# Gate/up jobs issued whole, the local part ahead of group 1, and the memory read-out behind the filler

## Chip, core and metric

The kernel runs on one core of a Trainium2 chip. The metric is the device time of one execution in microseconds. A run's time is a little longer than the span of its profile, which begins with the first recorded instruction.

## What is computed

One transformer block on 2048 tokens of width 448, in bf16. A condition vector gives six modulation vectors; the block is an attention with memory, then a gated MLP, each behind a modulated LayerNorm and each added to its input:

```python
mod = (_silu(c) @ w_mod).reshape(c.shape[0], 6, 1, -1)
h = _layernorm(x, axis=-1) * (1 + ca) + sa
x = x + ga * _A_ref(h, A_wq, A_wk, A_wv, A_wo, A_beta)
h = _layernorm(x, axis=-1) * (1 + cb) + sb
x = x + gb * _B_ref(h, B_w_gate, B_w_up, B_w_down)
```

The attention has 16 heads of 28 and works on 4 segments of 512 tokens. In each segment the output of a head is a mix of two parts. The local part is a causal softmax attention in the segment. The memory part reads a matrix M and a vector z, which sum phi(k) v and phi(k) over the earlier segments, with phi(q):

```python
num = jnp.einsum('bhld,bhde->bhle', pq, M)
den = jnp.einsum('bhld,bhd->bhl', pq, z)[..., None] + 1e-06
o = g * (num / den) + (1.0 - g) * a_dot
M = M + jnp.einsum('bhld,bhle->bhde', pk, vs)
```

The MLP computes `(sigmoid(h @ w_gate) * (h @ w_up)) @ w_down`, with 1792 inner columns.

## The kernel before

The order of the instructions is written out by hand. One list of jobs, `fill`, holds the PE work that isn't softmax attention: projections, memory updates, wo tiles, gate/up jobs and down tiles, each with an estimated cost in ns. A main loop (lines 697 to 737) goes over the 4 segments `s`, in each over 4 units `hc` (four heads each), and in each unit over three logits groups `g`. After each group `run_fill` (582) takes jobs from the list until the pace of the segment is used up. `later` and `tick` (76, 88) put off small operations of DVE, POOL and ACT by an estimated time, so that they stand later in the queues.

- `logits` (401) makes one group: matmuls for four heads side by side into the one PSUM tile `lg` (four banks), then one exponential on ACT (417). Groups 0 and 1 are 512 columns wide per head (group 1 as 384 + 128), group 2 is 256. A new group can start only when the exponential of the one before has read `lg`. After group 0 from segment 1 on, `phi` (359) makes an exponential of the unit's queries on ACT, and two DVE operations (365, 366) later.
- `mask` (423) runs on POOL.
- `pv` (428) is the local part of the unit before: 40 matmuls `acc` (439), then on DVE r1 (445, 446), t1 (451) and ou (452).
- `mem_read` (456) is the memory read-out of the unit before: 4 matmuls `mem` (463), then on DVE r2 (466, 467) and t2 (470). `otr` (481) issues the transpose of the result to oT on the SP queue.
- `wo_tile` (490): 4 matmuls `pwo`, on DVE the sum with x (497), the LN statistics, and later xn (267, 270); its transpose to hT goes over SP (276). The modulation (280) follows on DVE.
- `gate_up` (512) makes the first part of a job for two of the 14 column blocks: 6 gate matmuls (519), then four short ones (524), two of them side by side in two halves of the array, the last rows of gate and of up; two tanhs on ACT (527). `gate_up2` (531) makes the other 6 up matmuls (536) and the two products fT on DVE (539).
- `down` (541): 14 matmuls `dps`, then the sum with x on DVE (549) and the output transfer.

Everything but `lg` shares four PSUM buffers (`ps_m`). A new tile takes one whose tile was released, and its first matmul waits for the operation that read it last. The projections' q and v copies are on ACT (342, 353), the k copy on DVE (344). `prep_b1` (591) puts off seven scalings of w_down by DVE (603).

Because the gate/up job is in two, a logits group and its exponential stand between its first part and its second: line 703 takes `gate_up2` right after a group, and `run_fill` goes on to a first part when a second part was the last it took. In segment 0, `prev` has no memory to read.

Of the kernel before, what the change touches and what calls it, by code (L numbers as in the profile page):

```python
# [17 lines left out]
def kernel(  # L18
# [23 lines left out]
    NFC = F // P  # L42
# [33 lines left out]
    def later(ns, fn, tag):  # L76
        deferred.append((clock[0] + ns, len(deferred), fn, tag))

    def run_deferred(pick):
        while True:  # L80
            due = [d for d in deferred if pick(d)]
            if not due:
                return
            d = min(due, key=lambda d: d[:2])
            deferred.remove(d)
            d[2]()

    def tick(ns):
        clock[0] += ns
        run_deferred(lambda d: d[0] <= clock[0])  # L90
# [154 lines left out]
    hT_of = {}  # L245
    MM, MV, TR = 216, 190, 60
    GU = 14 * MM + 200
# [111 lines left out]
    def phi(src, wait, tag, then=None):  # L359
        e = work.tile([P, L], BF16, tag="e", bufs=5, name="e")  # L360
        nc.scalar.activation(e[:], src, AF.Exp)

        def fin():
            r = work.tile([P, L], BF16, tag="r", bufs=2, name="r")
            nc.vector.tensor_scalar(r[:], src, 0.0, 1.0, op0=ALU.max, op1=ALU.add)
            nc.vector.tensor_tensor(e[:], e[:], r[:], ALU.min)
            if then:
                then(e)
        later(wait, fin, tag)
        return e  # L370
# [28 lines left out]
    pT_of, pq_of, ou_of, oT_of = {}, {}, {}, {}  # L399

    def logits(s, hc, g):
        u = (s, hc)
        qT, kT = qT_of[s], kT_of[s]
        if g == 0:
            pT_of[u] = pipe.tile([P, 4, PTW], BF16, tag="pT", bufs=2, name="pT")
        pT = pT_of[u]
        lg = ps_lg.tile([P, 4, 512], F32, tag="lg", name="lg")
        w0 = OFF[KB_GROUPS[g][0]]
        wid = 0
        for kb in KB_GROUPS[g]:  # L410
            nq = L - kb * P
            for hs in range(4):
                r = slice(HP * hs, HP * hs + Dh)
                nc.tensor.matmul(lg[:, hs, wid:wid + nq], lhsT=kT[r, hc, kb * P:(kb + 1) * P],  # L414
                                 rhs=qT[r, hc, kb * P:L], start=True, stop=True, tile_position=(HP * hs, 0))
            wid += nq
        nc.scalar.activation(pT[:, :, w0:w0 + wid], lg[:, :, 0:wid], AF.Exp, scale=scale)  # L417
        if g == 0 and s > 0:
            pq_of[u] = phi(qT[:, hc, :], 3600, ("pq", u))
        for kb in KB_GROUPS[g]:  # L420
            later(2600, lambda kb=kb: mask(pT, kb), ("mask", u))

# [33 lines left out]
    def mem_read(s, hc):  # L456
        u = (s, hc)
        mem = m_f32("mem")
        memv = mem[:].rearrange("p (t h e) -> p t h e", h=4, e=HP)
        need(("pq", u), ("rm", s))  # L460
        pq = pq_of.pop(u)
        for qb in range(TPS):
            nc.tensor.matmul(memv[:, qb, :, 0:ME], lhsT=pq[:, qb * P:(qb + 1) * P], rhs=rm_of[s][:, hc, :, :],  # L463
                             start=True, stop=True)
        r2 = work.tile([P, TPS, 4], F32, tag="r2", bufs=2)
        nc.vector.scalar_tensor_tensor(r2[:], memv[:, :, :, Dh], 1e-6, cb(1, hc), op0=ALU.add, op1=ALU.mult)
        nc.vector.reciprocal(r2[:], r2[:])
        t2 = work.tile([P, TPS * 4, Dh], F32, tag="t2", bufs=2)
        t2_of[u] = t2
        nc.vector.tensor_tensor(t2[:], num(mem), bc(r2), ALU.mult)  # L470
# [10 lines left out]
    def otr(s, hc):  # L481
        ou = ou_of.pop((s, hc))
        if hc == 0:
            oT_of[s] = pipe.tile([P, NHC, TPS, P], BF16, tag="oT", bufs=1, name="oT")
        nc.sync.dma_start_transpose(oT_of[s][:, hc, :, :], ou[:].rearrange("p t h e -> p (t h e)"))
# [21 lines left out]

    fT_of = {}

    half = {}  # L510

    def gate_up(s, f0):
        h = hT_of[("2", s)]
        fcs = (f0, f0 + 1)
        fs = [slice(fc * P, (fc + 1) * P) for fc in fcs]
        gp = [m_f32("gps") for _ in fcs]
        for g, f in zip(gp, fs):
            for k in range(3):
                nc.tensor.matmul(g[:, 0:L], lhsT=wg_sb[:, k, f], rhs=h[:, k, :], start=(k == 0), stop=False)  # L519
        up = [m_f32("ups") for _ in fcs]  # L520
        tts = []
        for g, u, f in zip(gp, up, fs):
            for dst, r, first in ((g, 0, False), (u, LW, True)):
                nc.tensor.matmul(dst[:, 0:L], lhsT=wgu_sb[r:r + LW, f], rhs=h[r:r + LW, 3, :], start=first,  # L524
                                 stop=not first, tile_position=(r, 0))
            tt = work.tile([P, L], F32, tag="tt", bufs=3)
            nc.scalar.activation(tt[:], g[:, 0:L], AF.Tanh, scale=0.5)  # L527
            tts.append(tt)
        half[0] = (s, fcs, up, fs, tts)

    def gate_up2():
        s, fcs, up, fs, tts = half.pop(0)
        h = hT_of[("2", s)]
        for fc, u, f, tt in zip(fcs, up, fs, tts):
            for k in range(3):
                nc.tensor.matmul(u[:, 0:L], lhsT=wu_sb[:, k, f], rhs=h[:, k, :], start=False, stop=(k == 2))  # L536
            ft = pipe.tile([P, L], BF16, tag="fT", bufs=NFC + 2, name="fT")
            fT_of[(s, fc)] = ft
            nc.vector.scalar_tensor_tensor(ft[:], tt[:], 1.0, u[:, 0:L], op0=ALU.add, op1=ALU.mult)  # L539
# [28 lines left out]
    def h2_jobs(s):  # L568
        return [(0, lambda: need(("ln2", s)))]

    def gu_jobs(s):
        jobs = []
        for fc in range(0, NFC, 2):
            jobs += [(GU - 6 * MM, lambda fc=fc: gate_up(s, fc)), (6 * MM, gate_up2)]
        return jobs

    def down_jobs(s):
        return [(NFC * MV, lambda t=t: down(s, t)) for t in range(TPS)]
# [1 line left out]
    fill = deque()  # L580

    def run_fill(ns):
        fn = None
        while fill and (ns > 0 or fn is gate_up2 and fill[0][0] == GU - 6 * MM):
            cost, fn = fill.popleft()
            fn()
            tick(cost)
            ns -= cost
        return ns
# [61 lines left out]
    m = [mem_jobs(s) for s in range(3)]  # L651
# [39 lines left out]
    def cost(jobs):  # L691
        return sum(cst for cst, _ in jobs)
# [3 lines left out]
    debt = 0.0  # L696
    for s in range(NSEG):
        for hc in range(NHC):
            prev = (s, hc - 1) if hc else (s - 1, NHC - 1)
            for g in range(3):  # L700
                logits(s, hc, g)
                tick(450)
                if fill and fill[0][1] is gate_up2:
                    fill.popleft()[1]()
                    tick(6 * MM)
                    debt -= 6 * MM
                if prev[0] > 0 and g == 0:
                    mem_read(*prev)
                    tick(250)
                if prev[0] >= 0 and g == 1:  # L710
                    pv(*prev)
                    tick(1000)
                if s >= 1 and hc == 1 and g == 0:
                    gj = gu_jobs(s - 1)
                    tail = list(fill)
                    print("left", s, cost(tail), len(tail))
                    fill.clear()
                    while tail and tail[0][1] is gate_up2:
                        fill.append(tail.pop(0))
                    for w in wo_jobs(s - 1):  # L720
                        fill.append(w)
                        if tail and s > 1:
                            fill.extend(tail[:2])
                            tail = tail[2:]
                    fill.extend(tail)
                    if s >= 2:
                        dj = down_jobs(s - 2)
                        fill.extend(dj[:3] + h2_jobs(s - 1) + dj[3:] + gj)
                    else:
                        fill.extend(h2_jobs(s - 1) + gj[:2] + m[2][0:1] + gj[2:10] + m[2][1:] + gj[10:])  # L730
                    pace[0] = (cost(fill) - KEEP[s] * GU) / (12 if s < 3 else 9)
                debt = run_fill(pace[0] + debt)
                if debt > 0:
                    print("dry", s, hc, g, debt)
                    debt = 0.0
                if prev[0] >= 0 and g == 2:
                    otr(*prev)
    last = NSEG - 1
    dj = down_jobs(last - 1)
    mem_read(last, NHC - 1)  # L740
    run_fill(2000)
    pv(last, NHC - 1)
    tick(1100)
    run_fill(1500)
    otr(last, NHC - 1)
    run_fill(3500)
    for c, fn in wo_jobs(last):
        fn()
        tick(c)
    fill.extend(dj)  # L750
    run_fill(1e9)
    for c, fn in h2_jobs(last) + gu_jobs(last) + down_jobs(last):
        fn()
# [30 lines left out]
```

## Time and profile before

| | us |
|---|---|
| median of 3 runs | 268.51 |
| the runs | 267.37, 268.51, 268.67 |
| the profiled execution | 267.37 |
| its span | 265.7 |

The profile has a page and answers drawn from its trace. A page's first part gives the busy time of each engine, the chain is the work that ended last, followed back from step to step. A timeline's row has the start, the time, the engine, the line, the operation with its output and inputs, and in brackets how long the engine was idle before it and what ended the wait. PE is TensorE, PEld its weight loads, DVE is VectorE, ACT is ScalarE, POOL is GpSimd, SP the queue of SyncE. A matmul row is drawn to its modelled end: matmuls of 512 columns take 380 ns in it, but follow each other after 215.

The stages of the span: up to about 28 us loading, LN and the first projections; to 90 us projections of the later segments as filler; to 201 us gate/up jobs, wo and down tiles of the segment before; after 201 us no logits are left, and the MLP of segment 3 is the end.

### The profile page before, as it was taken

To read this page: it belongs to the slowest core of one execution; us is meant where nothing else is said; L and a number is where in the kernel's file an instruction comes from. 1 tells how busy PE (TensorE), PEld (TensorE's weight loads), DVE (VectorE), ACT (ScalarE), POOL (GpSimd) and SP (SyncE) were. 2 spreads that over 40 slices of the span, in tenths; PEclk is the share of its full clock that TensorE was granted. 3 is DMA by queue.
4 is the path that set the end of the run, shared out by engine and by line. 5 is a ranking of instruction groups with operands and counts; after the bars stand their busy time and mean duration, and the time that the engine had idled before them with its cause. 6 is when DMAs were issued, how large, how long until landed. Compare 5 with 4: busy or idle time off the path is not lost.

```text
span 265.7 us, 5242 instructions
## 1 busy us (share of the span) xinstructions
PE 241.1 (91%) x2030; PEld 113.3 (43%) x2054; DVE 183.4 (69%) x431; ACT 137.8 (52%) x169; POOL 70.8 (27%) x130
## 2 busy tenths in 40 slices
PE   7798799979496999898999999899999999999995
PEld 2434344534242443453544343445443445433352
DVE  5789898956489868888976575896765568444421
ACT  0569589948436697883617658533572210133300
POOL 3229323522244313343422131243230013000000
PEclk9999999988999999999999999999999999999999
DMA  5999568296901202300232000013200003300011
GB/s 153 278 238 271 177 139 172 38 208 158 184 22 42 54 8 42 60 21 20 58 62 55 20 20 2 20 23 94 57 1 20 22 0 61 89 0 0 2 35 35
DMA packets 40992, 19.66 MB, mean 74 GB/s; under 512 B 29704, under 2 KB 40072, under 8 KB 40968
## 3 DMA queue, kind: packets, MB, share of 16 engines
q1 hardware_dynamic: 39320, 18.36, 30.7%
q10 hardware_dynamic: 1648, 0.98, 1.4%
q8 instruction: 16, 0.26, 0.4%
q14 instruction: 8, 0.07, 0.1%
HBM read 10.67 MB, written 1.84 MB: 47 GB/s over the span
## 4 chain that ended last, share of the span: by engine, by line
PE 43%; DVE 6%; ACT 2%; issue 2%; DMA 1%; POOL 0%; DVEq 0%
PE dps L545 14%; PE ups L536 10%; PE gps L519 9%; PE gps L524 4%; PE acc L439 2%; PE pwo L494 2%; DVE fT L539 1%; PE lg L414 1%; ACT pT L417 1%; DVE ot L549 1%; DMA hT<-xn 1%; ACT tt L527 1%; DVE t L451 1%; DVE hT L280 1%; PE mem L463 1%
## 5 line engine op out<-in xcount | busy, mean ns | idle before, releaser
L417 ACT ACTIVATE pT<-lg 128x2048 bf16<-128x2048 f32 (+1 forms) x48 | 76.8, 1600 | 32.6 <-PE lg L414 32.5
L425 POOL TENSOR_SCALAR_AFFINE_SELECT pT<-pT 128x512 bf16<-128x512 bf16 x64 | 42.6, 681 | 68.9 <-ACT pT L417 68.9
L527 ACT ACTIVATE tt<-gps 128x512 f32<-128x512 f32 x56 | 30.4, 595 | 56.1 <-PE gps L524 56.1
L539 DVE SCALAR_TENSOR_TENSOR fT<-tt,ups 128x512 bf16<-128x512 f32 x56 | 36.9, 685 | 31.4 <-PE ups L536 27.5
L545 PE MATMUL dps<-wd_sb,fT 128*128 128x448 bf16 x224 | 43.7, 352 | 0.1
L536 PE MATMUL ups<-hT,wu_sb 128*128 128x512 bf16 x166 | 40.7, 381 | 0.2 <-issue 0.2
L519 PE MATMUL gps<-hT,wg_sb 128*128 128x512 bf16 x154 | 39.8, 379 | 0.8 <-issue 0.2
L545 PEld LDWEIGHTS <-fT 128*128 128x128 bf16 x224 | 21.6, 98 | 20.1 <-issue 0.2
L263 POOL TENSOR_SCALAR rs<-mv 128x1 f32<-128x1 f32 (+2 forms) x21 | 5.4, 256 | 72.7 <-DVE mv L260 69.4
L519 PEld LDWEIGHTS <-wg_sb 128*128 128x128 bf16 x168 | 15.9, 98 | 17.7
L536 PEld LDWEIGHTS <-wu_sb 128*128 128x128 bf16 x168 | 14.2, 98 | 21.1 <-issue 7.1
L259 DVE BATCH_NORM_STATS2 st<-x_sb 128x6 f32<-128x448 bf16 x32 | 19.7, 617 | 3.4 <-DMA x_sb<-in_A_x_dram 2.8
L414 PE MATMUL lg<-qT,kT 28*128 28x512 bf16 (+3 forms) x256 | 17.4, 305 | 3.1 <-ACT pT L417 2.8
L339 PE MATMUL pq<-hT,wq_sb 128*128 128x512 bf16 x60 | 16.8, 379 | 3.4 <-DVE hT L298 2.8
L524 PE MATMUL ups<-hT,wgu_sb 64*128 64x512 bf16 x56 | 17.6, 381 | 2.1 <-DVE x_sb L497 1.5
L439 PEld LDWEIGHTS <-pT 128*128 128x128 bf16 x640 | 17.5, 96 | 4.3 <-issue 2.9
L267 DVE TENSOR_SCALAR xn<-x_sb,mv,rs 128x448 bf16<-128x448 bf16 x32 | 16.0, 519 | 4.6 <-POOL rs L264 4.6
L439 PE MATMUL acc<-vt,pT 128*128 128x29 bf16 x640 | 18.6, 175 | 0.5 <-ACT tt L527 0.5
L549 DVE TENSOR_TENSOR ot<-dps,x_sb 128x448 bf16<-128x448 f32 x16 | 9.8, 619 | 11.4 <-PE dps L545 9.4
L339 PE MATMUL pq<-hT,wk_sb 128*128 128x512 bf16 x61 | 16.3, 380 | 0.9 <-ACT qT L342 0.5
L524 PE MATMUL gps<-hT,wgu_sb 64*128 64x512 bf16 x56 | 17.0, 381 | 0.1
L351 PE MATMUL pv<-wv_sb,hT 128*128 128x448 bf16 x64 | 15.1, 380 | 2.0 <-DVE kT L344 2.0
(89 smaller groups left out, 256.6 us busy)
## 6 DMA issues: line engine op xcount, KB each, us to landing
wm<-in_w_mod_dram SPq DMA_DIRECT2D x5, 392.0 KB, 8.2
out_dram<-ot SPq DMA_DIRECT2D x16, 112.0 KB, 1.7
x_sb<-in_A_x_dram SPq DMA_DIRECT2D x3, 448.0 KB, 4.7
wd_sb<-in_B_w_down_dram SPq DMA_DIRECT2D x3, 448.0 KB, 9.5
wg_sb<-in_B_w_gate_dram SPq DMA_DIRECT2D x3, 448.0 KB, 3.7
wu_sb<-in_B_w_up_dram SPq DMA_DIRECT2D x3, 448.0 KB, 5.9
wm<-in_w_mod_dram ACTq DMA_DIRECT2D x1, 392.0 KB
wo_sb<-in_A_wo_dram SPq DMA_DIRECT2D x4, 98.0 KB
```

The source lines that it names most:

```text
L259: nc.vector.bn_stats(st[:], self.srcs[i])
L339: nc.tensor.matmul(pq[:, 0:L], lhsT=head_cols(w_sb, k, hc), rhs=h[:, k, :], start=(k == 0), stop=(k == NK - 1))
L414: nc.tensor.matmul(lg[:, hs, wid:wid + nq], lhsT=kT[r, hc, kb * P:(kb + 1) * P], rhs=qT[r, hc, kb * P:L], start=True, stop=True, tile_posi ...
L417: nc.scalar.activation(pT[:, :, w0:w0 + wid], lg[:, :, 0:wid], AF.Exp, scale=scale)
L425: nc.gpsimd.affine_select(out=blk, in_=blk, compare_op=ALU.is_ge, fill=0.0, base=0, pattern=[[0, 4], [1, P]], channel_multiplier=-1)
L439: nc.tensor.matmul(accv[:, qb, hs, 0:ME], lhsT=pT[:, hs, c0:c0 + P], rhs=vt[:, kb, hc * 4 + hs, 0:ME], start=(kb == 0), stop=(kb == qb))
L519: nc.tensor.matmul(g[:, 0:L], lhsT=wg_sb[:, k, f], rhs=h[:, k, :], start=(k == 0), stop=False)
L524: nc.tensor.matmul(dst[:, 0:L], lhsT=wgu_sb[r:r + LW, f], rhs=h[r:r + LW, 3, :], start=first, stop=not first, tile_position=(r, 0))
L527: nc.scalar.activation(tt[:], g[:, 0:L], AF.Tanh, scale=0.5)
L536: nc.tensor.matmul(u[:, 0:L], lhsT=wu_sb[:, k, f], rhs=h[:, k, :], start=False, stop=(k == 2))
L539: nc.vector.scalar_tensor_tensor(ft[:], tt[:], 1.0, u[:, 0:L], op0=ALU.add, op1=ALU.mult)
L545: nc.tensor.matmul(dp[:, 0:D], lhsT=fT_of[(s, fc)][:, t * P:(t + 1) * P], rhs=wd_sb[:, fc, :], start=(fc == 0), stop=(fc == NFC - 1))
```

## The change

The diff has these parts.

1. `gate_up` makes the whole job again, first the 6 gate matmuls, the four short ones and the tanhs, then the 6 up matmuls and the products. `gate_up2`, the jobs of two pieces, and what handles them in `run_fill` and the loop are gone.
2. The local part of the unit before (`pv`) stands ahead of the logits of group 1, not behind.
3. The memory read-out (`mem_read`) stands behind the filler of group 0, not ahead of it.
4. The DVE part of phi for the queries is put off by 4500, not 3600.
5. At the end: a fill time of 6000 in place of 1500, of 3000 in place of 3500, and two of the four down tiles of segment 2 are put on the list ahead of the last wo tiles.

```diff
-            pq_of[u] = phi(qT[:, hc, :], 3600, ("pq", u))
+            pq_of[u] = phi(qT[:, hc, :], 4500, ("pq", u))
...
-        half[0] = (s, fcs, up, fs, tts)
-
-    def gate_up2():
-        s, fcs, up, fs, tts = half.pop(0)
-        h = hT_of[("2", s)]
         for fc, u, f, tt in zip(fcs, up, fs, tts):
...
-        jobs = []
-        for fc in range(0, NFC, 2):
-            jobs += [(GU - 6 * MM, lambda fc=fc: gate_up(s, fc)), (6 * MM, gate_up2)]
-        return jobs
+        return [(GU, lambda fc=fc: gate_up(s, fc)) for fc in range(0, NFC, 2)]
...
-                logits(s, hc, g)
-                tick(450)
-                if fill and fill[0][1] is gate_up2:
-                    fill.popleft()[1]()
-                    tick(6 * MM)
-                    debt -= 6 * MM
-                if prev[0] > 0 and g == 0:
-                    mem_read(*prev)
-                    tick(250)
                 if prev[0] >= 0 and g == 1:
                     pv(*prev)
                     tick(1000)
+                logits(s, hc, g)
+                tick(450)
...
                 if prev[0] >= 0 and g == 2:
                     otr(*prev)
+                if prev[0] > 0 and g == 0:
+                    mem_read(*prev)
+                    tick(250)
...
     pv(last, NHC - 1)
     tick(1100)
-    run_fill(1500)
+    run_fill(6000)
     otr(last, NHC - 1)
-    run_fill(3500)
+    fill.extend(dj[:2])
+    run_fill(3000)
     for c, fn in wo_jobs(last):
         fn()
         tick(c)
-    fill.extend(dj)
+    fill.extend(dj[2:])
```

The number of matmuls, and of instructions on the other engines, is the same. The order of PE's jobs in three places (G is a job's first part, U its second, lg0 to lg2 the groups, q and k projections, v the value projections):

```
segment 1, its first wo tiles
before: lg0 mem wo wo wo lg1 acc wo k q lg2 k q lg0 mem k v v lg1 acc v v
after:  lg0 wo wo wo mem acc lg1 wo k q lg2 k q lg0 k v v mem acc lg1 v v

then the first gate/up jobs
before: G lg2 U lg0 mem G lg1 U acc G lg2 U G lg0 U mem lg1 acc G lg2 U dM lg0 mem wo G lg1 U acc wo
after:  GU lg2 lg0 GU mem acc lg1 GU lg2 GU lg0 mem acc lg1 GU lg2 dM lg0 wo GU mem acc lg1 wo

after the last logits group
before: lg2 GU G mem U G acc U GU GU wo wo wo wo, four down tiles, seven GU, four down tiles
after:  lg2 GU mem GU acc GU GU GU wo wo wo wo, four down tiles, seven GU, four down tiles
```

More of the change, by code (lines that the diff above doesn't have):

```diff
@@ L508 @@
     fT_of = {}
-    half = {}
     def gate_up(s, f0):
@@ L582, in run_fill @@
     def run_fill(ns):
-        fn = None
-        while fill and (ns > 0 or fn is gate_up2 and fill[0][0] == GU - 6 * MM):
+        while fill and ns > 0:
             cost, fn = fill.popleft()
@@ L717 @@
                     fill.clear()
-                    while tail and tail[0][1] is gate_up2:
-                        fill.append(tail.pop(0))
                     for w in wo_jobs(s - 1):
@@ L722 @@
                         if tail and s > 1:
-                            fill.extend(tail[:2])
-                            tail = tail[2:]
+                            fill.append(tail.pop(0))
                     fill.extend(tail)
@@ L729 @@
                     else:
-                        fill.extend(h2_jobs(s - 1) + gj[:2] + m[2][0:1] + gj[2:10] + m[2][1:] + gj[10:])
+                        fill.extend(h2_jobs(s - 1) + gj[:1] + m[2][0:1] + gj[1:5] + m[2][1:] + gj[5:])
                     pace[0] = (cost(fill) - KEEP[s] * GU) / (12 if s < 3 else 9)
```

## The prediction

> **What bounds the kernel now.** I read the page's busy shares first, then the chain that ended last, then the timelines of PE, DVE and ACT from 70 us on.
>
> ```profile
> PE 241.1 (91%) x2030; PEld 113.3 (43%) x2054; DVE 183.4 (69%) x431; ACT 137.8 (52%) x169; POOL 70.8 (27%) x130
> PE 43%; DVE 6%; ACT 2%; issue 2%; DMA 1%; POOL 0%; DVEq 0%
> ```
>
> PE bounds the kernel. The second line is the chain, which is only traced back to 119 us; in that part PE is on it nearly everywhere, and DVE and ACT only where PE waits. The number of matmuls doesn't change, so the change is worth what it does to PE's waits. These are the waits that it touches (PE timeline; in brackets the idle time and its releaser):
>
> ```profile
> 72.72 2.33 PE L494 MATMUL pwo<-wo_sb,oT 128*128 128x448 bf16 x10 [1.87 <-DMA oT<-ou]
> ...
> 84.38 0.92 PE L351 MATMUL pv<-wv_sb,hT 128*128 128x448 bf16 x4 [0.94 <-DVE kT L344]
> 86.35 0.92 PE L351 MATMUL pv<-wv_sb,hT 128*128 128x448 bf16 x4 [1.05 <-DVE kT L344]
> ...
> 93.93 0.40 PE L414 MATMUL lg<-qT,kT 28*128 28x512 bf16 x4 [0.25 <-ACT pT L417]
> ...
> 101.56 0.39 PE L524 MATMUL ups<-hT,wgu_sb 64*128 64x512 bf16 x1 [0.52 <-DVE t L451]
> ...
> 108.13 0.40 PE L414 MATMUL lg<-qT,kT 28*128 28x384 bf16 x8 [0.78 <-ACT pT L417]
> ...
> 123.24 0.37 PE L524 MATMUL ups<-hT,wgu_sb 64*128 64x512 bf16 x1 [0.75 <-DVE x_sb L497]
> ...
> 153.07 0.40 PE L414 MATMUL lg<-qT,kT 28*128 28x384 bf16 x8 [0.78 <-ACT pT L417]
> ...
> 161.52 0.40 PE L414 MATMUL lg<-qT,kT 28*128 28x512 bf16 x4 [0.25 <-ACT pT L417]
> ...
> 171.14 0.37 PE L524 MATMUL ups<-hT,wgu_sb 64*128 64x512 bf16 x1 [0.80 <-DVE x_sb L497]
> ...
> 202.31 0.37 PE L463 MATMUL mem<-rm,e 128*128 128x116 bf16 x4 [0.47 <-ACT tt L527]
> ...
> 206.28 1.15 PE L439 MATMUL acc<-vt,pT 128*128 128x29 bf16 x40 [0.47 <-ACT tt L527]
> ```
>
> The bracket understates a wait, because the matmul before it is drawn to its modelled end. I therefore use starts: four L524 matmuls take 0.53 us in the chain (0.32 and 0.21), but 1.44 at 100.44 to 101.88, 1.65 at 121.89 to 123.54 and 1.80 at 169.65 to 171.45. Those waits are 0.9, 1.1 and 1.3.
> The Trainium skill ("Trainium Kernel Development and Optimization", Performance Expectations) calls matmul busy time a bad metric because matmuls are pipelined. By the brackets the three removals are 2.1 us and the sum below +2.7; by the starts they are 3.3 and the sum +1.5.
>
> Durations used, all from this trace: one gate/up job 3.23 (1.29 gate + 0.53 + 1.40 up), memory read-out 0.22 to 0.32, local part 1.05, one wo tile 0.76, the dM matmuls 0.94. Exponentials: 1.88 and 1.03. Tanh: 0.55. From the start of a 256-wide logits group (134.06) to its exponential is 0.34 (134.40); with 1.02 for it and 0.04 until PE goes on, the next group can start 1.40 after it.
>
> **To 72.7 us: nothing.** The local part goes ahead of group 1, ACT's total stays the same, and the first wo matmuls wait for the oT transposes, which SP issues from 51.18 to 68.97 without a gap. Those stand in the same order on SP, but for one pk transpose that passes one hT transpose. Without that cover, a reordering of ACT would cost up to its 0.74 at 46.83. I take 0.
>
> **73 to 92 us, the DVE queue: +2.1.** DVE works here almost without a pause:
>
> ```profile
> 70.00:80.00 10.00, 7.53 (x85) 3.82 (x83) 7.63 (x21) 5.61 (x6) 4.55 (x9) 1.00 0.45 46
> 80.00:90.00 10.00, 7.66 (x84) 3.88 (x82) 9.49 (x24) 6.63 (x8) 4.25 (x7) 1.00 0.24 56
> ```
>
> (Columns: stretch, length, PE, PEld, DVE, ACT, POOL busy, clock, DMA.) Before, the first read-out's three DVE instructions (70.51 to 71.55) and one w_down scaling (71.55) ran while PE waited for oT. Afterwards both stand behind the first wo sums: 1.03 + 0.55 = 1.58 us more ahead of the kT copies, for which PE waits at 84.38 and 86.35. The second read-out (86.76) moves behind the third kT copy, ahead of the last hT modulation, and the first gate tile of the next job gets its PSUM buffer. Walking the queue, the first gate matmul moves from 90.06 to about 91.7: +1.65. The modulations also need the last hT transpose, for which the walk uses the median landing, 2.6 us from issue. From the end of the last xn copy to the first modulation it took 3.6 and 3.7 at 133.04 to 136.63 and 180.66 to 184.36, with an output transfer ahead on SP, which doesn't stand there now; that would make it +2.6. I take 2.1, halfway, because SP's issues stand close here too. Lower bound -0.5: the kT waits of 2.0 go, but hT's landing keeps most of it.
>
> **Group 2 straight before group 0 (first gate/up unit): +0.8.** Before, 1.40 us of up matmuls lay between the two and 0.25 was still waited. Now nothing does: 1.40 minus the group's 0.22 is 1.2, less 0.4 for what is waited and lost there today.
>
> **Group 2 with only dM or one wo tile behind it: +0.7.** 1.40 minus 0.22 minus 0.94 is 0.25; with 0.76 it is 0.42. Before, the 1.40 us of up matmuls covered both.
>
> **Read-out and local part right after a gate/up job: +0.9.** Their PSUM buffers are those of the two tanh inputs (L527). After group 0, ACT has its exponential (1.88) and one of phi (0.6) ahead of the tanhs; the first time also one of kT. The walk gives 0.7 there, and 0.1 at each of the two later jobs of that kind. Bounds 0.3 and 1.5.
>
> **Waits at 101 and 108: -1.1.** 0.9 goes, because PE has a whole job between a local part and the last L524. The 0.8 at 108 stays as 0.65: 1.27 of read-out and local part lie behind group 0 instead of up matmuls and read-out, and the exponential no longer stands behind two tanhs.
>
> **Waits at 123 and 171: -0.2.** 1.1 + 1.3 go. In their place, t1 (L451) now has the read-out's 1.03 and phi's 0.7 ahead of it on DVE, and the last up tile gets the buffer of the same job's first gate tile, so it waits for its tanh: 0.85 to 1.45 each, depending on whether xn and its copy take 0.5 (as at 178.09) or 1.13 (165.80 to 166.93). I take 1.1 each.
>
> **144 to 162: -0.5.** 0.2 at 153 and 0.3 at 161, where a whole job now covers group 2's exponential.
>
> **After the last logits group: -1.2.** Four waits go: 0.16, 0.47, 0.47 and about 0.3 at 210.5. The read-out and the local part follow whole jobs, whose tanhs are done. Bounds -1.4 and -0.7. The other numbers of fill time and the two down tiles put in early change nothing: in the built order, gate/up jobs use the time up, and all four down tiles still stand behind the last wo tile. They cover the last LN as before, just so: its modulation starts at 228.08, the gate matmuls at 228.96. If two had gone ahead, 5.3 us of that cover would be missing.
>
> Sum: 2.1 + 0.8 + 0.7 + 0.9 - 1.1 - 0.2 - 0.5 - 1.2 = **+1.5 us**. The profiled execution took 267.37 (span 265.7 and 1.7 around it) and would take 268.9. It is the fastest of the three runs; their median is 268.51, so I predict **270.0**.
>
> **The clock.** The granted clock is 1.00 from 70 to 90 us in the rows above, with waits of 0.94, 1.05 and 1.87 in them, so I take no loss from the new waits.
> The Trainium skill ("TensorE: Matmul & The Clock Gate", Part 1) puts PE at half rate after an idle window of about 3.4 us; by an estimate from that page one such window would add 1.7 us to the sum. No wait that I expect is that long.
>
> **Rivals.**
> - *Even.* The hT transposes land in 2.6 us and xn is quick: 1.65 and -0.7 for the terms 2.1 and -0.2, so +0.6, and with the tanh term at its lower 0.3 it is 0.0: 268.5 to 269.1. For it: I walked the queue to 1.65. Against: xn took 0.69, not 0.36, where POOL worked beside it. 0.36.
> - *Faster.* One mechanism: DVE's queue is less full than I walk it, as the wo sums and LN steps pack closer. The kT copies are then on time at 84, and t1 at 122 and 170. The 73 to 92 term is its lower bound, -0.5, and at 123 and 171 only the tanh wait of 0.3 each is left: -1.8. Sum -2.7: 265.8. It decides from the point where DVE idles over 1.6 us between 74 and 86, but the trace shows it idle there only 0.2. 0.12.
> - *DVE behind for longer.* The backlog reaches the next LN and the gate jobs at 140 and 188 wait for hT: 2.6 for the first term, 0.5 at 123 and 171, tanh 1.5: +3.3 to +4: 272. Against: hT is ready 2 us before 140 and 0.7 before 188. 0.15.
> - *As forecast*, +1 to +2.5: 0.37.
>
> By these cases, with the even one's edge and the forecast's lower edge inside 0.5% (1.34 us, about what a measurement of this kernel tells from no change: the three runs lie 0.49% apart): faster 0.12, same 0.38, slower 0.50. The range leaves out most of the faster case (0.09) and what the last one has above 272.5 (0.06): 266.9 to 272.5; the likeliest case's own is 269.5 to 271.
>
> **What would show it.** The first gate matmul 1.6 to 2.6 later than 90.06, behind DVE; a wait of about 1.2 between group 2 and group 0 after it; waits of mem and acc on tt; no wait of PE between the last logits and the last wo. The prediction is wrong if the first gate matmul comes before 91, or if the time past 188 doesn't shrink by about 1.

## The result, and the profile after

The changed kernel took 271.95 us (median of 4 runs, 271.51 to 272.43), the kernel before, run beside it, 267.94 (4 runs, 267.26 to 268.67): a ratio of 1.015 (1.0111 to 1.0188). Repeated (e5 below) it took 270.33 against 268.28: 1.0082 (1.0058 to 1.0105). So it is slower, by 2 us or by 4; most of the difference between the two goes with PE's clock, as e1 shows. The profiled execution took 272.43 us with a span of 270.7. Busy shares and the chain of its page:

```profile
PE 245.1 (91%) x2029; PEld 115.4 (43%) x2054; DVE 184.1 (68%) x431; ACT 137.7 (51%) x169; POOL 70.0 (26%) x130
...
PE 62%; DVE 16%; DMA 9%; ACT 7%; issue 4%; SPq 1%; POOL 1%; ACTq 0%; DVEq 0%
```

PE still bounds it and does the same matmuls, but is busy 4 us longer; three more stretches at half clock in this execution (see e1) can account for that. DVE's part of the chain went from 6% to 16%; the two aren't quite alike, because this chain is traced back to the start. The waits that answer to those shown of before, in the timeline of PE:

```profile
75.17 3.35 PE L494 MATMUL pwo<-wo_sb,oT 128*128 128x448 bf16 x10 [2.57 <-DMA oT<-ou]
...
82.93 1.04 PE L339 MATMUL pq<-hT,wq_sb 128*128 128x512 bf16 x4 [0.91 <-DVE t L470]
...
90.12 0.37 PE L463 MATMUL mem<-rm,e 128*128 128x116 bf16 x4 [0.81 <-DVE kT L344]
...
94.13 1.47 PE L517 MATMUL gps<-hT,wg_sb 128*128 128x512 bf16 x5 [0.70 <-DVE t L470]
...
99.01 0.40 PE L414 MATMUL lg<-qT,kT 28*128 28x512 bf16 x4 [1.13 <-ACT pT L417]
...
102.96 0.37 PE L463 MATMUL mem<-rm,e 128*128 128x116 bf16 x4 [0.22 <-ACT tt L525]
...
114.41 0.40 PE L414 MATMUL lg<-qT,kT 28*128 28x384 bf16 x8 [0.73 <-ACT pT L417]
...
128.69 0.37 PE L522 MATMUL ups<-hT,wgu_sb 64*128 64x512 bf16 x1 [0.22 <-ACT tt L525]
...
136.76 0.82 PE L439 MATMUL acc<-vt,pT 128*128 128x29 bf16 x26 [0.50 <-POOL pT L425]
...
160.90 0.40 PE L414 MATMUL lg<-qT,kT 28*128 28x384 bf16 x8 [0.73 <-ACT pT L417]
```

In the kernel before, the first gate matmul has no wait:

```profile
90.06 1.46 PE L519 MATMUL gps<-hT,wg_sb 128*128 128x512 bf16 x5
```

Three things are to be seen. The first gate matmul comes at 94.13 instead of 90.06, and the last thing that it waits for is the read-out's t (L470), whose PSUM buffer it takes; a q projection waits for the same at 82.93. Group 2 is followed straight by group 0, and PE waits 1.13 for the exponential. The waits for x_sb and t1 at 101, 123 and 171 are gone or shorter, and past the last logits no PE wait is drawn any more. The DVE timeline shows why the read-out is late. Before, its t (L470) comes ahead of the first wo sum (L497):

```profile
71.00 0.62 DVE L470 TENSOR_TENSOR t<-mem,r 128x448 f32<-128x448 f32 x1
...
73.58 0.62 DVE L497 TENSOR_TENSOR x_sb<-pwo,x_sb 128x448 bf16<-128x448 f32 x1 [1.42 <-PE pwo L494]
```

Afterwards:

```profile
79.86 0.62 DVE L497 TENSOR_TENSOR x_sb<-pwo,x_sb 128x448 bf16<-128x448 f32 x1
...
82.25 0.62 DVE L470 TENSOR_TENSOR t<-mem,r 128x448 f32<-128x448 f32 x1
...
91.99 1.06 DVE L280 TENSOR_SCALAR hT<-hT,cols 128x512 bf16<-128x512 bf16 x3 [0.79 <-DMA hT<-xn]
...
93.45 0.62 DVE L470 TENSOR_TENSOR t<-mem,r 128x448 f32<-128x448 f32 x1
93.99 0.60 DVE L280 TENSOR_SCALAR hT<-hT,cols 128x512 bf16<-128x512 bf16 x1
```

Its instructions stand behind three wo sums with their LN steps (the third ends at 81.9), and the second one stands between the hT modulations that the gate matmuls need.

### The profile page after: what moved, and what is told of

Same layout as the page of the kernel before. It is cut to its first block, busy times and chain, and to the rows that moved or that the text cites. A ratio compares the mean times of both kernels' runs of the same rounds, so it can differ in the third digit from the quotient of the medians.

```text
span 270.7 us, 5234 instructions
## 1 busy us (share of the span) xinstructions
PE 245.1 (91%) x2029; PEld 115.4 (43%) x2054; DVE 184.1 (68%) x431; ACT 137.7 (51%) x169; POOL 70.0 (26%) x130
## 4 chain that ended last, share of the span: by engine, by line
PE 62%; DVE 16%; DMA 9%; ACT 7%; issue 4%; SPq 1%; POOL 1%; ACTq 0%; DVEq 0%
PE dps L538 15%; PE ups L529 13%; PE gps L517 12%; PE pq L339 6%; PE gps L522 5%; DMA wm<-in_w_mod_dram 4%; ACT pT L417 4%; PE lg L414 3%; PE acc L439 3%; DMA hT<-xn 3%; PE pwo L494 2%; DVE st L259 2%; DMA oT<-ou 2%; DVE xn L267 2%; DVE x_sb L497 1%
## 5 line engine op out<-in xcount | busy, mean ns | idle before, releaser
L425 POOL TENSOR_SCALAR_AFFINE_SELECT pT<-pT 128x512 bf16<-128x512 bf16 x64 | 41.5, 664 | 76.3 <-ACT pT L417 76.3
L517 PEld LDWEIGHTS <-wg_sb 128*128 128x128 bf16 x168 | 15.2, 98 | 19.4 <-issue 1.7
L339 PE MATMUL pq<-hT,wq_sb 128*128 128x512 bf16 x60 | 18.0, 410 | 3.9 <-DVE hT L298 2.6
L439 PEld LDWEIGHTS <-pT 128*128 128x128 bf16 x640 | 18.3, 96 | 2.7 <-issue 1.3
L494 PE MATMUL pwo<-wo_sb,oT 128*128 128x448 bf16 x64 | 15.2, 374 | 2.7 <-DMA oT<-ou 2.6
L267 DVE TENSOR_SCALAR xn<-x_sb,mv,rs 128x448 bf16<-128x448 bf16 x32 | 15.4, 498 | 0.4 <-POOL rs L264 0.4
```

The lines of the kernel that those rows point to most:

```text
L339: nc.tensor.matmul(pq[:, 0:L], lhsT=head_cols(w_sb, k, hc), rhs=h[:, k, :], start=(k == 0), stop=(k == NK - 1))
L425: nc.gpsimd.affine_select(out=blk, in_=blk, compare_op=ALU.is_ge, fill=0.0, base=0, pattern=[[0, 4], [1, P]], channel_multiplier=-1)
L439: nc.tensor.matmul(accv[:, qb, hs, 0:ME], lhsT=pT[:, hs, c0:c0 + P], rhs=vt[:, kb, hc * 4 + hs, 0:ME], start=(kb == 0), stop=(kb == qb))
```

## The experiments

All times are medians; e1 to e4, e5 to e8 and e9 to e12 ran on one chip each, with the kernel before among them (268.12, 268.28 and 268.98 us).

### How far do runs of one kernel lie apart?

**e1**: the kernel before, unchanged.

> The kernel before, unchanged, to see how far its time and its mean granted clock move by themselves. The changed kernel's profile is 2.45 us behind already at the first wo tiles (75.17 for 72.72), 0.7 of it before 28 us where the order is the same, with granted clocks of 0.83 to 0.93 from 10 to 40 us where the profile of before has 1.00. Theory A (the early clock is chance, the same for both kernels): the mean clock here spreads from about 0.975 to 0.995 and the time by 1 to 2 us. Theory B (the changed order makes the clock fall): the clock here stays at 0.99 or more in nearly all runs, ratio 1.000.

268.79 us against 268.12, ratio 1.0017 (0.9986 to 1.0049): no difference, as it must be. But its 12 runs go from 266.87 to 270.25, and 22 of the other set's 23 from 266.40 to 269.77 (one took 270.54): 1.4% in all, not the 0.49% that I had read from three runs. Part of this goes with the mean granted clock, which moves in steps. Below is e9's trace by single microseconds (columns: stretch, length, PE, PEld, DVE, ACT, POOL busy, PE's clock, DMA share, GB/s), where the matmuls had just resumed at 108.94 after a wait of 1.72 us:

```profile
109.00:110.00 1.00, 1.00 (x37) 0.79 (x37) 0.06 (x1) 1.00 (x2) 0.59 (x1) 1.00 0.62 123
110.00:111.00 1.00, 0.95 (x20) 0.57 (x18) 0.46 (x3) 1.00 (x1) 0.00 (x0) 0.90 0.37 82
111.00:112.00 1.00, 1.00 (x4) 0.30 (x2) 0.96 (x2) 0.26 (x1) 0.67 (x2) 0.50 0.27 58
...
114.00:115.00 1.00, 1.00 (x6) 0.29 (x3) 0.27 (x1) 0.20 (x1) 0.00 (x0) 0.89 0.22 46
```

The clock is either 1.00 or 0.50, and a half-rate stretch is 3.4 us long here and in every profile of this case (once, in e12, two follow each other), so one costs at most 1.71 us of matmul work. It begins after PE is at work again here, and mostly. In the 14 profiles one began in, or within 3.4 us behind, 22 of the 26 PE waits of 2.0 us or more and 9 of the 38 from 1.2 to 2.0 (without the wait that every run starts with).

Which waits do it isn't chance alone. In every profile the stretches begin on a grid of 3.413 us, counted from the first record of the clock: in the changed kernel's profile this record is at 4.64, and its stretches, at 11.47, 28.54, 59.26 and 76.32, begin 2, 7, 16 and 21 steps later. I leave out the 39 steps that hold the one-column matmuls of the condition vector. Of the others, PE was drawn idle for 47% or more (the share that parts the two kinds best here) in 26, and 24 of these were followed by a step at half rate; of the 1016 with less idle time none was. So a wait counts by how much of one step it fills: e9's wait of 1.72 us fell nearly whole into the step from 107.38 to 110.80, and half rate began at 110.80. The grid starts at another point in every execution, and that is what is left to chance.

The Trainium skill ("TensorE: Matmul & The Clock Gate", Part 1) has this as a gate at half or full rate, judged over free-running windows of about 3.4 us, and asks for one idle window of that length; the length of a stretch and the grid agree, but here a window about half idle has been enough.

A mean clock of 0.994, 0.987, 0.981 and 0.975 is then about one, two, three and four stretches: (1 − clock) × span / 1.71. For the kernel before the mean times of 10, 23, 29 and 7 runs with so many are 267.4, 268.1, 268.7 and 269.2 us. Fitted by a line, one costs 0.61 us and not 1.71; some fall where PE would wait anyway (e8 shows such a place). The line explains about a third of the runs' variance; the rest stays open. This allows a second reading of each kernel below: **its time less that of the kernel before with as many stretches** ("at equal clock", with twice the standard error). For the changed kernel that is +2.65 ± 0.34 over both sets of runs (10 runs): +2.92 in the first, whose runs had three or four stretches, and +2.47 in e5, with one or two. It leaves out what a kernel's own waits do to the clock: the mean number of stretches is 2.5 in the kernel before, 2.4 in the changed one, but 4.2 in e4 and 4.8 in e12.

### Which part of the change costs the time?

**e3**: the read-out goes back ahead of the filler, the rest stays.

```diff
                 logits(s, hc, g)
                 tick(450)
+                if prev[0] > 0 and g == 0:
+                    mem_read(*prev)
+                    tick(250)
...
-                if prev[0] > 0 and g == 0:
-                    mem_read(*prev)
-                    tick(250)
```

> The changed kernel with the memory read-out back ahead of the filler of group 0. Theory (the read-out's DVE work in the full DVE queue at 73 to 92 costs 1.6 us, and its wait for tanh 0.7, and 0.2 at each of two later jobs): 1.5 to 2.5 us faster than the changed kernel, ratio to before 1.006 to 1.010. Rival (DVE isn't what delays the first gate matmul, but the clock and the later oT landing): ratio 1.013 to 1.016.

267.86 us, ratio 0.9988 (0.9959 to 1.0018); at equal clock +0.01 ± 0.24. With the read-out early the whole loss is gone: the other four parts together are worth nothing. In PE's timeline the first gate matmul has no wait any more. The second read-out now waits 1.40 for phi (L366), whose DVE part part 4 puts off further; before, it waited 0.35, and not for phi:

```profile
73.15 2.32 PE L494 MATMUL pwo<-wo_sb,oT 128*128 128x448 bf16 x10 [1.39 <-DMA oT<-ou]
...
83.67 0.39 PE L463 MATMUL mem<-rm,e 128*128 128x116 bf16 x4 [1.40 <-DVE e L366]
...
90.22 1.61 PE L517 MATMUL gps<-hT,wg_sb 128*128 128x512 bf16 x5
```

From the first of these rows to the last it is 17.07 us; before it was 17.34, in the changed kernel 18.96. So the wait for phi costs nothing in this stretch. Whether the other parts would gain without part 4 wasn't tried.

**e6** and **e7**: only the two read-outs that fall beside the first wo tiles go back ahead (e6), or only those two stay late (e7).

```diff
e6, behind the logits, and then in the late place (e7: the two conditions exchanged)
+                if prev[0] > 0 and g == 0 and prev in ((1, 0), (1, 1)):
+                    mem_read(*prev)
+                    tick(250)
...
-                if prev[0] > 0 and g == 0:
+                if prev[0] > 0 and g == 0 and prev not in ((1, 0), (1, 1)):
```

> The changed kernel with only the two read-outs between 70 and 92 us (of segment 1, units 0 and 1) ahead of the filler; the other ten stay behind it. Theory (the DVE queue at 73 to 92 us and the wait for oT ahead of it are the cost): recovers 2.5 to 3.5 of the 4 us, ratio 1.002 to 1.006. Rival (the waits of later read-outs for tanh, and later DVE queues, cost the most): recovers 1 or less, ratio 1.011 or more.

> The complement: only those two read-outs behind the filler, the other ten ahead of it. Theory: loses 2.5 to 3.5 us against the version with all read-outs early, ratio 1.008 to 1.012. Rival: 1.000 to 1.004. If the two parts don't add up to the 4 us, they act on each other.

e6 took 268.69, ratio 1.0012 (0.999 to 1.0034), at equal clock +0.78 ± 0.38. e7 took 269.94, ratio 1.0061 (1.0037 to 1.0085), at equal clock +1.79 ± 0.40. They add up: 0.78 + 1.79 = 2.57 of 2.65. The two read-outs at the wo tiles are worth 1.8 us, the other ten 0.8. I had expected 2.5 to 3.5 for the two, since I counted from 4 us, which held what the clock had added.

**e5**: the changed kernel again, to stand beside them.

> The changed kernel, unchanged, on this chip and beside the others: 271 to 272.5 us, ratio 1.011 to 1.016. Its mean granted clock, 0.975 to 0.981 in four runs, against 0.974 to 0.994 in 35 runs of the kernel before: if the late read-out draws the clock down, it stays at or below 0.985 here; if that was chance, it spreads as widely as before's.

270.33 us, as told above, at a clock of 0.986 to 0.994: the late read-out doesn't draw it down. It is 1.64 above e6, which ran beside it. Wo to first gate matmul: 73.54 to 92.51, 18.97.

**e2** and **e4**: the local part goes back behind group 1, in segment 0 only (e2) or everywhere (e4).

```diff
e2:
-                if prev[0] >= 0 and g == 1:
+                if s > 0 and g == 1:
                     pv(*prev)
                     tick(1000)
                 logits(s, hc, g)
                 tick(450)
+                if s == 0 and prev[0] >= 0 and g == 1:
+                    pv(*prev)
+                    tick(1000)
e4: the same block behind the logits in all segments
```

> The changed kernel with the local part behind group 1 in segment 0 only, as before the change; all that differs lies before about 62 us. Theory B (the order there costs time or clock): recovers 1.5 to 2.4 us, ratio to before about 1.007 to 1.009. Theory A (chance): no more than 0.3 us away from the changed kernel, ratio 1.014 to 1.016.

> The changed kernel with the local part behind group 1 everywhere, as before the change. Theory (ahead of group 1 it covers 1.05 us of the exponential of group 0 where no filler stands between; behind it, two waits of 0.73 grow to 1.8, but PE's order before 62 us is that of before): about even with the changed kernel if the early loss is chance, +2 us, ratio 1.020; if the early loss comes from this part, ratio 1.010 to 1.014.

e2 took 271.21, ratio 1.0113 (1.0075 to 1.015). This ratio alone can't tell the two theories apart. At equal clock it is +2.83 ± 0.46 beside the changed kernel's 2.65 ± 0.34, so the local part's new place in segment 0 shows no cost, to within about 0.6 us. e4 took 274.61, ratio 1.0228 (1.0184 to 1.0272): with late read-outs and whole jobs, the local part ahead of group 1 saves about 1%.

### Is it DVE's queue, or PE's clock, behind the first wo tiles?

In the profiles of the changed kernel the clock is at half rate just behind the wait for oT (its wo matmuls take 3.35 us instead of 2.33), so it could be the clock that makes the first gate matmul late.

**e8**: eight matmuls whose result nothing uses stand ahead of the first wo tiles and keep PE at work in that wait.

```diff
+    def keep_busy():
+        kb_ = m_f32("kb")
+        for _ in range(8):
+            nc.tensor.matmul(kb_[:, 0:D], lhsT=ident[:], rhs=wv_sb[:, 0, :], start=True, stop=True)
...
+                    if s == 1:
+                        fill.append((0, keep_busy))
                     for w in wo_jobs(s - 1):
```

> The changed kernel with 8 more matmuls of 448 columns (1.5 us, result unused) ahead of the first wo tiles, where PE waits 2 to 2.6 us for the oT transposes. Theory C (the longer wait lets the granted clock fall, 0.83 from 70 to 80 us, and the ten wo matmuls behind it take 3.35 instead of 2.33): the clock stays, 0.7 to 1.2 us faster than the changed kernel. Theory D (the DVE queue behind the wo sums sets the first gate matmul, whatever the clock): within 0.3 us of the changed kernel.

271.0 us, ratio 1.0107 (1.0084 to 1.0129); at equal clock +3.10 ± 0.38. Its PE timeline:

```profile
71.03 1.69 PE L687 MATMUL kb<-wv_sb,ident 128*128 128x448 bf16 x8
...
73.44 2.32 PE L494 MATMUL pwo<-wo_sb,oT 128*128 128x448 bf16 x10 [0.34 <-DMA oT<-ou]
...
78.78 1.02 PE L339 MATMUL pq<-hT,wk_sb 128*128 128x512 bf16 x3 [0.63 <-DVE x_sb L497]
...
81.19 1.04 PE L339 MATMUL pq<-hT,wq_sb 128*128 128x512 bf16 x4 [1.38 <-DVE t L470]
...
92.38 1.47 PE L517 MATMUL gps<-hT,wg_sb 128*128 128x512 bf16 x5 [0.69 <-DVE t L470]
```

The clock stayed up (2.32 for the wo matmuls, where e5 has 3.56), and the 1.2 us won there are waited at the projections, for DVE. From wo to the first gate matmul it is 18.94, as without. The queue sets this stretch; the clock is hidden in it. By medians e8 is 0.67 above e5, more than the 0.3 that theory D allowed, though their intervals overlap. Their two profiles don't show it: from the first gate matmul to the last local part both take 115.55 us.

### What are the other parts worth alone?

**e9**: whole jobs alone, with the read-out early and the local part behind group 1. **e10**: the local part ahead of group 1 alone, put into the kernel before.

```diff
e9 (from the changed kernel)
                 logits(s, hc, g)
                 tick(450)
+                if prev[0] > 0 and g == 0:
+                    mem_read(*prev)
+                    tick(250)
+                if prev[0] >= 0 and g == 1:
+                    pv(*prev)
+                    tick(1000)
     and both blocks out of their new places
e10 (from the kernel before)
+                if prev[0] >= 0 and g == 1:
+                    pv(*prev)
+                    tick(1000)
                 logits(s, hc, g)
     and the block out of its old place
```

> Whole gate/up jobs as in the changed kernel, but the read-out ahead of the filler and the local part behind group 1, as before the change: against the version with the read-out early (ratio 0.999) it shows the worth of the local part's place where the jobs are whole. Theory (with whole jobs, nothing stands between group 0 and group 1 at two places but read-out and local part; behind group 1 the local part no longer covers 1.05 us there): 2 to 3 us slower than with the local part ahead, ratio 1.006 to 1.011. Rival (the local part's place is worth nothing, the whole jobs as such are even): ratio 0.997 to 1.002.

> The kernel before with only the local part ahead of group 1; the gate/up jobs stay in two pieces, the read-out early. Theory (it covers 1.05 us of the two waits of 0.78 at 108 and 153, and the oT wait sets the time before): 0.5 to 1.5 us faster than before, ratio 0.994 to 0.998. Rival (it only delays group 1's exponential, which ends just as late): 0.999 to 1.003.

Each alone loses (e9 keeps parts 4 and 5, e10 has neither). e9 took 270.62, ratio 1.0073 (1.0044 to 1.0102); e10 took 271.88, ratio 1.0103 (1.0067 to 1.0138), 2.9 us slower where I had expected a gain. Together (e3) they are even. PE's timeline of e9:

```profile
106.50 0.40 PE L414 MATMUL lg<-qT,kT 28*128 28x512 bf16 x4
106.83 0.39 PE L463 MATMUL mem<-rm,e 128*128 128x116 bf16 x4
108.94 0.40 PE L414 MATMUL lg<-qT,kT 28*128 28x384 bf16 x8 [1.72 <-ACT pT L417]
109.27 1.17 PE L439 MATMUL acc<-vt,pT 128*128 128x29 bf16 x40
110.29 2.25 PE L517 MATMUL gps<-hT,wg_sb 128*128 128x512 bf16 x5
```

Between groups 0 and 1 only the read-out is left to cover an exponential of 1.88 us; the local part between them would be 1.1 us of cover, and in e3 the wait is 0.73. The half-rate stretch shown above comes on top: the five gate matmuls take 2.25 us instead of 1.47. The same happens at 157.96, and at both places in e4. And e10, where the local part follows the first part of a job whose tanh isn't done, so that its PSUM buffer isn't free:

```profile
98.02 1.16 PE L439 MATMUL acc<-vt,pT 128*128 128x29 bf16 x40 [1.40 <-ACT tt L527]
```

The same wait is 0.89 at 144.19 and 0.46 to 0.47 at three more places. So the order of the local part is worth what stands around it, and no number can be given for it alone.

### Is there a better version?

**e11**: e3, with one filler job between any two groups, to cover the waits of 1.13 and 0.73 for the exponential. **e12**: e11, with two projection jobs ahead of the first wo tiles, to cover the wait for oT.

```diff
e11:
-                debt = run_fill(pace[0] + debt)
+                debt = run_fill(max(pace[0] + debt, 1.0 if s else -1e9))
e12 also:
+                    if s == 1:
+                        fill.extend(tail[:2])
+                        tail = tail[2:]
                     for w in wo_jobs(s - 1):
```

> The changed kernel with the read-out ahead of the filler, and from segment 1 on at least one job behind every logits group, so that no two groups stand without filler between them. If the waits of PE for exponentials with whole jobs (1.13, 0.73, 0.73 and 0.2 to 0.3) are what is left: 1.5 to 2.5 us faster than the version with the read-out early, ratio 0.990 to 0.994. If earlier jobs only bring other waits (LN of the next segment, DVE): 0.997 to 1.001.

> The version before this one, with two projection jobs of segment 2 and 3 ahead of the first wo tiles, in PE's wait for the oT transposes (1.3 to 2.6 us). If that wait delays PE: 1 to 1.7 us faster still, ratio 0.984 to 0.990. If the DVE queue behind the wo sums sets the first gate matmul: no gain, as the wo sums move later by as much, ratio within 0.002 of the version before this one.

e11 took 270.33, ratio 1.0067 (1.0036 to 1.0097), e12 273.8, ratio 1.0186 (1.0154 to 1.0218). Both ideas fail. In e11 the waits for the exponential are gone, and two longer ones have come, in a trace that was 1.1 us ahead of e3's at the first gate matmul and 2.7 behind at the last local part:

```profile
130.51 0.58 PE L463 MATMUL mem<-rm,e 128*128 128x116 bf16 x4 [2.80 <-DVE e L366]
...
181.10 0.83 PE L439 MATMUL acc<-vt,pT 128*128 128x29 bf16 x26 [2.30 <-POOL pT L425]
```

PE has used its filler before and comes to the read-out and the local part sooner than phi (L366) and POOL's mask of pT are done there, and each of these waits was followed by a half-rate stretch. In e12 the wait for oT is gone, but the first wo tile comes 1.6 us later than in e11, and the four sums on DVE 1.2, 5.0, 4.6 and 2.3 later, in a queue that sets the stretch anyway: the first gate matmuls wait for hT's modulation (0.37, 0.26 and 0.45 us). No kernel here beats the one before by more than its uncertainty.

## Why the prediction was right, and where its terms were not

I forecast 270.0 us, 1.5 above the kernel before; it is 2.0 to 4.0 by medians and 2.65 at equal clock. The direction and the first cause were right; the sum was about 1.1 us too small. Section by section, by starts in the two traces (before 72.72, 90.06, 93.93, 109.48, 139.68, 161.52, 187.88, 265.7; after 75.17, 94.13, 99.01, 114.74, 146.22, 168.13, 193.86, 270.7), with the change in the number of PE's switches, which are explained below:

| section (time of before) | predicted | measured | switches |
|---|---|---|---|
| to 72.7 | 0 | +2.45 (mostly chance) | |
| 73 to 90, the DVE queue | +2.1 | +1.62 | |
| first group 2 to group 0 | +0.8 | +1.01 | −1 |
| to 109 (tanh +0.7, 101 and 108 −1.1) | −0.4 | +0.18 | +3 |
| to 140 (dM and wo +0.7, 123, a tanh) | +0.8 | +1.28 | +3 |
| to 162 | −0.5 | +0.07 | +4 |
| to 188 (171, a tanh) | −0.1 | −0.63 | +1 |
| past 188 | −1.2 | −0.98 | +1 |
| sum past 72.7 | +1.5 | +2.55 | +11 |

- **To 72.7 us, nothing: right.** The 2.45 are mostly chance: the two traces already differ by 0.7 at 28 us, with the same instructions up to there; the same wo matmuls start at 73.81 in e1's trace of the kernel before and at 73.54 in e5's of the changed one; and e2 finds no cost of the new order in segment 0. This pair held a before trace with one stretch (mean clock 0.994) and a changed one with four (0.975). That is also where much of the first ratio of 1.015 came from.
- **"I take no loss from the new waits": right on average, for a wrong reason.** The changed runs have as many stretches as those of before (2.4 and 2.5). But I read the gate as one that needs about 3.4 us of waiting, and looked at 70 to 90 us only; the trace of before has a stretch itself, at 58.11.
- **73 to 92 us, the DVE queue: right**, cause and place; the walk's 1.65 was better than the 2.1 that I took (from wo to the first gate matmul the changed traces take 18.96 and 18.97, those of before 17.34 and 17.64; 1.8 by e7). I had expected the longer wait for hT's transposes; the modulation waited 0.79 for them, but ran while the read-out's t was still awaited. I hadn't seen that a q projection would wait for the same buffer.
- **Group 2 straight before group 0: right** (+1.01 for +0.8). The two smaller cases, dM and one wo tile, were 0.18 and 0.27 by the brackets.
- **Read-out and local part after a gate/up job: right in kind.** At 102.96 and 103.45 they wait 0.38 and 0.27 by starts for the tanhs: 0.65, for 0.7.
- **Waits at 101 and 108: over-sized.** 0.9 at 101 became 0.2; that at 108 stayed, as I had said (0.73 by its bracket). That is −0.8 instead of −1.1.
- **144 to 162: half missed.** The wait at 161 is gone, but that at 153 is hardly less (0.73 for 0.78 by the brackets, where I had taken 0.2 off), and this section has four more switches, 0.4 us.
- **123 and 171: right in kind**; the waits that took their place are 0.85 by starts at 128.69, at the lower end of my 0.85 to 1.45.
- **Missed: the local part's wait for POOL's mask**, 0.50 at 136.76 (1.21 in e3's trace, 0.79 in e9's). The traces of before have no such wait. It can't be the local part's new place alone: e9, with the local part in its old place, has the wait, and so have all versions with whole jobs but e4, while e10 has none. Why is open.
- **Missed, and the largest: a group inside a job is cheaper than one between jobs.** Compare PE's timeline of the kernel before

```profile
96.10 0.38 PE L524 MATMUL ups<-hT,wgu_sb 64*128 64x512 bf16 x1
96.41 0.40 PE L414 MATMUL lg<-qT,kT 28*128 28x384 bf16 x8
96.74 1.47 PE L536 MATMUL ups<-hT,wu_sb 128*128 128x512 bf16 x6
98.04 1.16 PE L439 MATMUL acc<-vt,pT 128*128 128x29 bf16 x40
```

with that of the changed one:

```profile
106.50 0.38 PE L522 MATMUL ups<-hT,wgu_sb 64*128 64x512 bf16 x1
106.80 1.47 PE L529 MATMUL ups<-hT,wu_sb 128*128 128x512 bf16 x6
108.20 0.29 PE L414 MATMUL lg<-qT,kT 28*128 28x256 bf16 x4
```

The six up matmuls take 1.30 us from start to start when a local part follows (6 × 0.216), and 1.40 when logits follow. Whenever the operand's rows change (128, 64 for the short ones, 28 for logits) PE loses 0.09 to 0.10 us; in both traces the least loss of all such switches is 0.089 and the median of each kind 0.092 to 0.101. A group between the short matmuls and U adds one switch (64, 28, 128 for 64, 128); a group between whole jobs adds two. From the first gate matmul on I count 99 in the kernel before and 110 in the changed one: 11 × 0.096 = 1.06 us, which is the missing sum. The switches are measured in the traces; that this is the missing time is reckoned, since all variants with whole jobs have 110 to 112, and none takes the switch by itself. That the sums fit so well is partly luck: the misses of the sections run from −0.5 to +0.6 us and partly cancel, and the switches are only some of each. The Trainium skill ("TensorEngine Tiling (Array Packing)", Tiling Modes, Key Properties) says that a change of tiling mode drains the engine; the rows above agree, if each of these row counts is a mode of its own, and give the price.
- **After the last logits group: right** (−0.98 for −1.2, and no wait is drawn). One of the four waits that I listed, 0.16 at 196.83, was none: that row has five of the six gate matmuls, and the record of the first, 0.2 us before, is missing.
- **The rivals.** "Even" rested on xn being quick, and the first term did come out as it said; "DVE behind for longer" didn't come: the gate jobs at 146 and 194 don't wait for hT. "Faster" didn't come either: DVE has no drawn pause from 76.0 to 91.2.

So the other parts, without the late read-out, were to bring 1.5 us (1.5 less 2.1 and 0.9), and brought nothing (e3): by this reckoning the switches, 1.06 us, are the largest part of what was missed, and the mask's wait is another.

## What to carry to other kernels

An instruction put behind other work is late on every engine that it feeds: before a read-out of 0.25 us on PE is moved behind filler, look at what its DVE steps will stand behind, and at who takes its PSUM buffer next. Whether a block belongs ahead of or behind another depends on what covers the waits around it: here two changes that lose 0.7% and 1.0% alone are even together. And before a time is read from one trace, count the half-rate stretches in it: two runs of one kernel differ by 0.6 us for each on average.

## What of the hardware was not expected

- Half-rate stretches of 3.4 us begin on a free-running grid of that step, mostly after the matmuls have resumed. Leaving out the steps with the condition vector's matmuls, 24 of the 26 steps in which PE was idle for 47% or more were followed by one, and none of the 1016 others. So a wait of 1.2 to 2.0 us is followed by one or not (9 of 38 were), depending on where it falls. From one stretch to four, the mean time of the kernel before goes from 267.4 to 269.2 us.
- Matmuls whose operand has other rows than the one before cost PE 0.09 to 0.10 us, in either direction, even where nothing waits. With some 100 switches past the first gate matmul, that is about 10 of this kernel's 268 us.
